# The last two weight pairs of an MLP's second linear by seven products too, in a fused LayerNorm, attention and MLP kernel

## Chip, cores and metric

One core of one Trainium2 chip. The metric is device time in microseconds of one execution, as the median of three runs. Numbers of the profile come from one further execution, taken by the hardware profiler.

## The reference

```
x = A_x                                   # [1, 2048, 576], fp32
xn = (x - mean(x)) / sqrt(var(x) + 1e-5)
qkv = xn @ wqkv                           # 32 heads of 18
# each token attends to 8 keys: itself and 7 earlier ones, 2 apart (masked before the start)
attn = softmax(q . k[pos - 2*w] / sqrt(18))
A = (sum over w of attn * v[pos - 2*w]) @ wo
h = xn @ w1 + b1                          # 576 -> 4608
B = (h * tanh(softplus(h))) @ w2          # Mish, 4608 -> 576
out = x + A + B
```

## The kernel before, in words

The 2048 tokens go in two halves of 1024 (hf 0 and 1), each in two blocks of 512. Every fp32 operand of a matmul is split in a high and a low part, so that one product takes three matmuls (high x high, high x low, low x high). The hidden 4608 columns go in 18 pairs q of 2 x 128 ("weight pairs"). Half 1 (hf = 0) prepares the weights: it loads them, splits them, and stores the split parts to DRAM (`keep`, `t_keep`); half 2 reads them back (`fetch`, `p_fetch`). Half 2 takes the pairs in the order Q1 = 1..17, 0, so the pair prepared first comes last.

Several products are done with seven half-size products in place of eight. In the second linear of half 2 this is done for groups of two pairs: the activations of the group form a 2 x 2 block matrix A11, A12, A21, A22 (by token block and 128 columns), the weights form B11, B21, B22 and four sums T1 to T4, and the left sides are A11, A12, A22 and four sums S1 to S4. Group e has seven "items" P1 to P7 in the order ORD = P7, P4, P1, P5, P2, P6, P3. For an item, `u_sum` makes the left sum in place, `u_high` (ACT) and `u_low` (DVE or POOL) split it into a unit u, `p_fetch` brings the weights (tile pw), and `p_item` does 24 matmuls 128x288 into four PSUM banks "po", which DVE adds to the sums accP. At the end `p_join` adds the seven sums up to the four outputs. Weight sums T1 to T4 are made in half 1 (`t_sum`, `t_high`, `t_low`, `t_keep`).

Eight groups (OC = 8) cover sixteen of the pairs. The last two pairs of half 2 (17 and 0) go by `m2_cols`: eight chunks of 24 matmuls, with split activations from `a_split`. Four of these chunks stand within the last pair, four after it, ahead of the output product with wo (`wo_part`, o_0 to o_7), whose left sides `o_split` transposes and splits.

Between the QKV products of half 2 and its first pair stands the z stage (`z_part`): the last QKV weights for four token blocks of 128, again by seven products. DVE adds their PSUM banks into zkv and zqs (`plus`), which frees the banks for the next products. At that time POOL and DVE also do the end of half 1's attention: POOL multiplies q by k (tiles pr_g_..), DVE reduces them to logits L, takes the maximum m and subtracts; then POOL multiplies by v (pv). POOL also makes sums s_62 to s_70 of the transposed input, which are split into S_1 and xt_1 (high and low) for later products.

The order of the program is set by a plan of slots: TensorE's work is a list of parts (`add`), and all else is put before a part by `before` and `put`, moved by a table MOVE of numbers by name; ON_VECTOR and ON_GPSIMD choose the engine of an addition. `spot(hf, q, i)` is a part within a pair; `at` finds a part. Attention is cut into steps spread over the parts that `ok` allows. Each engine runs its instructions strictly in program order. SP issues the DMAs. PSUM has four banks with tag "h" and four with tag "out".

Of the kernel before, what the change touches and what calls it, by code (L numbers as in the profile page):

```python
# [31 lines left out]
OC = 8  # L32
# [12 lines left out]
def block_kernel(ctx: ExitStack, tc: tile.TileContext, x, wq, wo, w1, b1, w2, mask, out):  # L45
# [239 lines left out]

    def fetch(kind, i):
        w = i
        if kind == "w2":
            w = 2 * Q1[i // 2] + i % 2
        elif kind != "wq":  # L290
            w = Q1[i]
# [410 lines left out]
    def prod(ph, wt, off, X, hi, lo, first, last):  # L702
        seq = [(off + k, wl, xs + k) for k in range(2) for wl, xs in ((0, hi), (0, lo), (1, hi))]
        for i, (wk, wl, xs) in enumerate(seq):
            nc.tensor.matmul(ph, wt[:, wl, wk * P:(wk + 1) * P], X[:, xs, :],  # L705
                             start=first and i == 0, stop=last and i == len(seq) - 1,
                             skip_group_check=True)
# [120 lines left out]

    def unit(e, k, qq):
        if (e, k, qq) not in units:  # L830
            units[e, k, qq] = sb.tile([P, 2, TB], F32R, tag=f"a{qq}", bufs=(3, 2)[qq], name=f"u_{e}_{k}_{qq}")
        return units[e, k, qq]

    def u_sum(e, k, qq):
        name, q = LEFT[ORD[k]], 2 * e + qq
        eng = engine(nc.gpsimd if (name, qq) in (("S1", 1), ("S4", 0)) else nc.vector, "u_sum", e, k, qq)
        x, y, op = dict(S3=("A11", "A21", ALU.subtract), S2=("A22", "S3", ALU.subtract), S1=("A11", "S2", ALU.add),
                        S4=("A12", "S2", ALU.subtract)).get(name, (None,) * 3)
        if x:
# [1 line left out]
            eng.tensor_tensor(out=t, in0=u_src(q, x), in1=u_src(q, y), op=op)
            held_[q, SLOT[name]] = name

    def u_high(e, k, qq):
        name, q = LEFT[ORD[k]], 2 * e + qq
        u = unit(e, k, qq)
        nc.scalar.copy(u[:, 0, :], u_src(q, name))

    def u_low(e, k, qq):
# [4 lines left out]
        eng.tensor_tensor(out=u[:, 1, :], in0=u_src(q, name),  # L854
                          in1=u[:, 0, :].bitcast(F32), op=ALU.subtract)

    def a_split(b, j):
        q = 2 * OC
        t = rawact[q, b, j]
        assert (q, f"A{b + 1}{j + 1}") in held_  # L860
        a = acts[1, q, b, j] = sb.tile([P, 2, TB], F32R, tag=f"a{b}", bufs=(3, 2)[b], name=f"act_1_{b}_{2 * q + j}")
        nc.scalar.copy(a[:, 0, :], t)
        nc.gpsimd.tensor_tensor(out=a[:, 1, :], in0=t, in1=a[:, 0, :].bitcast(F32), op=ALU.subtract)
# [50 lines left out]
    def m2_cols(hf, q, b, p):
        for c in range(2):
            for r_ in range(2):
                po = ps.tile([P, 512], F32, tag="out", bufs=4, name=f"po_{hf}_{q}_{b}_{p}_{c}_{r_}")[:, 0:HC]
# [643 lines left out]
```

## Time and profile before

| | |
|---|---|
| median of 3 runs | 1109.08 us (1108.84 to 1109.54) |
| profiled execution, own time | 1108.86 us |
| its span | 1106.9 us |
| granted TensorE clock, mean | 0.998 |
| TensorE busy | 1097.6 us, 6534 matmuls |
| VectorE (DVE) busy | 864.5 us |
| GpSimd (POOL) busy | 818.3 us |
| ScalarE (ACT) busy | 509.6 us |

The span is what the trace covers; some 2 us lie around it. PE is TensorE's matmuls, PEld its weight loads, which run beside them. In a row of groups, "out<-in" names the tiles, the shapes are partitions x elements, then follow the count, busy time, mean ns of one, and the idle time before with what ended it. In a timeline row stand the start, the time, the engine, the line and the operation.

### The profile page before, as it was taken

The page shows a single profiled execution, that of the slowest core. Times are in us where ns is not written, and L with a number is a line of the kernel's source. Part 1 is how long each engine was busy: PE and PEld are TensorE (multiplying, and loading weights), DVE is VectorE, ACT ScalarE, POOL GpSimd, SP SyncE. Part 2 cuts the span into 40 slices and gives each one's busy share as a digit, 9 for nine tenths or more (in the row PEclk, how much of TensorE's full clock was granted, in tenths as well). Part 3 has the DMA queues.
Part 4 walks back from the last instruction along what each step waited for, and adds up shares of the span by engine and source line. Part 5 has one row for each costly group of instructions (what it writes and reads, how often), then busy time and mean ns, then how long its engine had stood idle before and what let it go on. Part 6 is the DMA issues. An engine that isn't in the chain of part 4 may idle for free.

```text
span 1106.9 us, 18216 instructions
## 1 busy us (share of the span) xinstructions
PE 1097.6 (99%) x6534; PEld 1012.0 (91%) x6534; DVE 864.5 (78%) x1419; ACT 509.6 (46%) x933; POOL 818.3 (74%) x659
## 2 busy tenths in 40 slices
PE   9999999999999999999999999999999999999998
PEld 8999999999999999999998889989989899999998
DVE  6258699999899898988745466777878879897876
ACT  5544655545456456546332264534444443434232
POOL 4499899876577776895888559868696868699622
PEclk9999999999999999999999999999999999999999
DMA  6789897988889788878589497666567765675653
GB/s 237 259 272 322 281 317 257 315 309 308 288 276 349 245 299 287 295 252 305 199 299 353 124 361 283 229 242 235 185 223 279 245 234 196 227 245 201 215 186 104
DMA packets 162957, 286.10 MB, mean 258 GB/s; under 512 B 30994, under 2 KB 102708, under 8 KB 162868
## 3 DMA queue, kind: packets, MB, share of 16 engines
q1 hardware_dynamic: 162868, 284.95, 74.3%
q8 instruction: 51, 0.84, 0.3%
q14 instruction: 38, 0.31, 0.1%
HBM read 168.35 MB, written 116.55 MB: 257 GB/s over the span
## 4 chain that ended last, share of the span: by engine, by line
PE 91%; POOL 3%; DVE 2%; DMA 1%; ACT 1%; issue 1%; POOLq 0%; ACTq 0%
PE h L705 31%; PE po L808 21%; PE po L900 16%; PE pq L359 8%; PE h L711 6%; PE o L1041 4%; PE z L477 2%; PE po L921 2%; POOL s L656 1%; POOL pr L582 1%; DVE og L626 0%; POOL pv L620 0%; DMA q_d<-qs 0%; DMA o_d<-og 0%; POOL s_u L656 0%
## 5 line engine op out<-in xcount | busy, mean ns | idle before, releaser
L808 PEld LDWEIGHTS po<-w,act 128*128 128x128 f32 x1728 | 236.5, 188 | 5.6
L808 PE MATMUL po<-w,act 128*128 128x288 f32 x1728 | 240.6, 295 | 0.0
L582 POOL TENSOR_TENSOR pr<-q,kv 128x576 f32<-128x576 f32 x128 | 192.5, 1532 | 12.3 <-DVE og L626 12.0
L620 POOL TENSOR_TENSOR pv<-L,kv 128x576 f32<-128x576 f32 x128 | 172.7, 1451 | 36.3 <-DVE L L613 13.1
L900 PEld LDWEIGHTS po<-pw,u 128*128 128x128 f32 x1344 | 184.0, 188 | 5.1 <-DVE u L854 0.5
L900 PE MATMUL po<-pw,u 128*128 128x288 f32 x1344 | 187.1, 295 | 0.1
L359 PE MATMUL pq<-wq,xt 128*128 128x432 f32 x672 | 136.3, 361 | 1.4 <-ACT xt L92 1.2
L812 DVE TENSOR_TENSOR acc<-po,acc 128x288 f32<-128x288 f32 x288 | 116.4, 447 | 21.2 <-PE po L808 20.2
L359 PEld LDWEIGHTS pq<-wq,xt 128*128 128x128 f32 x672 | 125.0, 188 | 8.2 <-ACT xt L92 1.8
L906 DVE TENSOR_TENSOR accP<-po,accP 128x288 f32<-128x288 f32 x212 | 89.0, 450 | 33.0 <-PE po L900 28.8
L705 PE MATMUL h<-xt,t 128*128 128x512 f32 x432 | 110.6, 391 | 0.0
L705 PE MATMUL h<-S,t 128*128 128x512 f32 x432 | 110.4, 391 | 0.0
L626 DVE TENSOR_REDUCE og<-pv 128x144 f32<-128x1152 f32 x64 | 85.7, 1342 | 26.8 <-POOL pv L620 26.7
L705 PE MATMUL h<-xt,wa 128*128 128x512 f32 x432 | 104.2, 390 | 0.0
L587 DVE TENSOR_REDUCE L<-pr 128x64 f32<-128x1152 f32 x64 | 85.9, 1344 | 19.0 <-POOL pr L582 18.6
L705 PEld LDWEIGHTS h<-xt,wa 128*128 128x128 f32 x432 | 81.0, 188 | 17.2
L705 PEld LDWEIGHTS h<-xt,t 128*128 128x128 f32 x432 | 79.0, 188 | 15.0 <-DVE c L750 0.2
L705 PEld LDWEIGHTS h<-S,t 128*128 128x128 f32 x432 | 78.1, 188 | 13.0
L761 POOL TENSOR_TENSOR act<-c,act 128x512 fp32r<-128x512 f32 x38 | 53.2, 1402 | 33.0 <-ACT act L756 33.0
L751 ACT ACTIVATE c<-c,b1c 128x512 f32<-128x512 f32 x57 | 41.3, 724 | 68.1 <-DVE c L750 68.0
L739 ACT COPY c<-h 128x512 f32<-128x512 f32 x57 | 33.3, 584 | 54.7 <-PE h L705 29.7
L705 PE MATMUL h<-S,wc 128*128 128x512 f32 x216 | 55.7, 393 | 0.7 <-ACT rt L739 0.7
(275 smaller groups left out, 1937.4 us busy)
## 6 DMA issues: line engine op xcount, KB each, us to landing
kv<-kv_d SPq DMA_DIRECT2D x64, 396.0 KB, 5.4
kept_t<-t SPq DMA_DIRECT2D x36, 512.0 KB, 4.8
t<-kept_t SPq DMA_DIRECT2D x36, 512.0 KB, 5.8
pw<-kept_T SPq DMA_DIRECT2D x32, 576.0 KB, 5.2
kept_B<-w SPq DMA_DIRECT2D x48, 288.0 KB, 4.7
pw<-kept_B SPq DMA_DIRECT2D x24, 576.0 KB, 4.8
rw<-in_w SPq DMA_DIRECT2D x36, 320.0 KB, 5.1
kept_wa<-wa SPq DMA_DIRECT2D x18, 640.0 KB, 5.4
```

The costliest lines, as they stand in the source:

```text
L359: nc.tensor.matmul(pq[:, 0:432], XT[:, xi, tok], wt[wi][:, hl, 0:432], start=i == 0, stop=i == len(seq) - 1)
L582: nc.gpsimd.tensor_tensor(out=pr[:, x:x + hh], in0=q[:, j0 + x:j0 + x + hh, None, :].to_broadcast([P, hh, W, CU]), in1=win(kt, 0, CU, j0 + ...
L587: nc.vector.tensor_reduce(L[:, k, j0:j0 + hj].rearrange("p j w h -> p (j w h)"), pr.rearrange("p j w (h d) -> p (j w h) d", h=2), axis=AX, ...
L620: nc.gpsimd.tensor_tensor(out=pr[:, x:x + hj].rearrange("p j d w -> p j w d"), in0=L[:, k, x:x + hj, :, h:h + 1].to_broadcast([P, hj, W, DH]),
L626: nc.vector.tensor_reduce(og[:, :, c0:c0 + DH], pr, axis=AX, op=ALU.add)
L705: nc.tensor.matmul(ph, wt[:, wl, wk * P:(wk + 1) * P], X[:, xs, :], start=first and i == 0, stop=last and i == len(seq) - 1, skip_group_ch ...
L711: nc.tensor.matmul(ph, wt[:, wl, off * P:(off + 1) * P], X[:, xs, :], start=False, stop=wl == 1, skip_group_check=True)
L761: engine(nc.gpsimd, "act", n).tensor_tensor(out=a[:, 1, :], in0=t, in1=a[:, 0, :].bitcast(F32), op=ALU.subtract)
L808: nc.tensor.matmul(po, acts[hf, q, b, j][:, al, tok], done["w2", hf, 2 * q + j][:, wl, c * HC:(c + 1) * HC], start=i == 0, stop=i == 5)
L812: nc.vector.tensor_tensor(out=t, in0=po, in1=t, op=ALU.add)
L900: nc.tensor.matmul(po, units[e, k, qq][:, al, tok], w[:, qq, wl, :], start=i == 0, stop=i == 5)
L906: nc.vector.tensor_tensor(out=t, in0=po, in1=t, op=ALU.add)
```

## The change

The ninth group. OC becomes 9, so the pairs 17 and 0 go by seven items as the others do, in an order of their own (LAST), and `m2_cols` and `a_split` go. All seven stand behind the last pair's first linear, four of them ahead of the transposes of `o_split`'s first steps and three behind.

```
-OC = 8
+OC = 9
...
-    seven = lambda hf, q: hf == 1 and q <= 2 * OC
+    seven = lambda hf, q: hf == 1
...
+    LAST = ("P1", "P4", "P7", "P5", "P2", "P6", "P3")
+    def nth(e, k):
+        return (LAST if e == OC - 1 else ORD)[k]
...
-    for k in range(4):
-        pr_(1, NP - 1, *CHUNKS[k])
+    while len(items) < 7 * OC:
+        pi()
...
+            if e == OC - 1:
+                ds = dict(P1=(0, -6, -5), P4=(0, -4, -3), P7=(-3, -2, -2), P5=(-2, -1, -1), P2=(0, -2, -2), P6=(-2, -2, -2),
+                          P3=(-3, -2, -1))[nth(e, k)]
...
-    for n, (a, b) in enumerate((("P6", "P1"), ("P7", "P6"), ("P6", "P5"), ("P2", "P1"), ("P3", "P6"), ("P4", "P7"), ("P5", "P7"))):
+    for n, (a, b) in enumerate((("P2", "P1"), ("P6", "P1"), ("P7", "P6"), ("P6", "P5"), ("P4", "P7"), ("P5", "P7"), ("P3", "P6"))):
         for pr in range(2):
...
+            i = items[-1][2] - 1 + (0, 0, 1, 1, 2, 3, 4)[n]
```

The weights of these pairs are now prepared as those of the others: sums T1 to T4 of the pairs 17 and 0 in half 1, kept in DRAM. Pair 0's w2 rows are loaded a second time for that, late in half 1 (`load_again`, at spot(0, 14, 8)), and its sums made at spot(0, 15, 8).

```
+    def load_again(i):
+        t = again["w2", i] = sb.tile([P, 5 * P], F32, tag="xn", bufs=XNB, name=f"again_{i}")[:, 0:D]
+        nc.sync.dma_start(t, w2[i * P:(i + 1) * P, :])
...
-    for q in range(1, 2 * OC + 1):
-        i = spot(0, q, (3,2)[q > 1])
+    for k in range(2):
+        before(spot(0, 14, 8) + k, lambda k=k: load_again(k))
+    for q in range(NP):
+        i = spot(0, q, (3, 2)[q > 1]) if q else spot(0, 15, 8)
```

Besides, o tiles 0 to 3 of the first half go to other buffers and are loaded within the last pair, wo's second part is fetched from the ninth group's third item on, attention steps may stand at every part of half 2, and the tables are set anew:

```
+    for i in range(spot(1, 0, 0), len(plan)):
+        ok[i] = True
...
-MOVE = {"0 s_high": -6, "0 s_low": 18, "0 s_step": 3, ...
+MOVE = {..., "u_sum 8 0 0": 77, "u_sum 8 0 1": 66, ...
```

**The tail on TensorE.** Before, these rows stand around the first transposes of `o_split` (ot_0), between the fourth and fifth chunk of the last pair; po_17 is a chunk's bank:

```order
L921 MATMUL po_17_1_1_1_1_11727<-w_1_0_11441,act_1_0_11564 128x288 x3
L921 MATMUL po_17_1_1_1_1_11727<-w_1_1_11368,act_1_1_11515 128x288 x3
L955 MATMUL ot_0_11740<-ident,o_1_11617 128x128 x4
L971 MATMUL ot_0_11741<-ident,o_0_11612 128x128 x4
L973 MATMUL ot_0_11742<-ident,o_0_11612 128x128
L973 MATMUL ot_0_11742<-ident,o_1_11617 128x128
L921 MATMUL po_17_0_0_0_0_11766<-w_1_0_11441,act_0_0_11396 128x288 x3
L921 MATMUL po_17_0_0_0_0_11766<-w_1_1_11368,act_0_1_11623 128x288 x3
```

After, the transposes stand between the fourth item (P5, po_3) and the fifth (P2, po_4) of the ninth group; the left sides come as weights pw against units u:

```order
L898 MATMUL po_3_1_1_11692<-pw_3_11481,u_3_0_11619 128x288 x3
L898 MATMUL po_3_1_1_11692<-pw_3_11481,u_3_1_11624 128x288 x3
L942 MATMUL ot_0_11710<-ident,o_1_11359 128x128 x4
L958 MATMUL ot_0_11711<-ident,o_0_11324 128x128 x4
L960 MATMUL ot_0_11712<-ident,o_0_11324 128x128
L960 MATMUL ot_0_11712<-ident,o_1_11359 128x128
L898 MATMUL po_4_0_0_11742<-pw_4_11664,u_4_0_11546 128x288 x3
L898 MATMUL po_4_0_0_11742<-pw_4_11664,u_4_1_11660 128x288 x3
```

With the seven items, 168 matmuls take the place of 192; the last pair's first linear before them is as it was.

**The z stage on DVE.** Before, from the second reduction of the logits of group 7 to the additions of token block 1 (z_1; the banks 7190 are the second product's):

```order
L587 TENSOR_REDUCE L_7_7111<-pr_7_0_1_7142 128x64
L587 TENSOR_REDUCE L_7_7111<-pr_7_1_0_7183 128x64
L490 TENSOR_TENSOR zkv_0_7082<-z_1_7192,zkv_0_7082 128x8x36
L490 TENSOR_TENSOR zqs_0_7083<-z_1_7192,zqs_0_7083 128x4x36
L587 TENSOR_REDUCE L_7_7111<-pr_7_1_1_7187 128x64
L597 TENSOR_TENSOR L_7_7111<-L_7_7111,mk 2x256
L601 TENSOR_REDUCE m_7_7217<-L_7_7111 128x32
L603 TENSOR_TENSOR L_7_7111<-L_7_7111,m_7_7217 128x256
L490 TENSOR_TENSOR zkv_1_7088<-z_1_7190,zkv_1_7088 128x8x36
L490 TENSOR_TENSOR zqs_1_7089<-z_1_7190,zqs_1_7089 128x4x36
```

After, from the first addition of token block 0 on:

```order
L491 TENSOR_TENSOR zqs_0_7126<-z_0_7135,zqs_0_7126 128x4x36
L588 TENSOR_REDUCE L_7_7024<-pr_7_0_1_7120 128x64
L588 TENSOR_REDUCE L_7_7024<-pr_7_1_0_7175 128x64
L491 TENSOR_TENSOR zkv_1_7131<-z_0_7133,zkv_1_7131 128x8x36
L491 TENSOR_TENSOR zqs_1_7132<-z_0_7133,zqs_1_7132 128x4x36
L491 TENSOR_TENSOR zkv_1_7127<-z_0_7134,zkv_1_7127 128x8x36
L491 TENSOR_TENSOR zqs_1_7128<-z_0_7134,zqs_1_7128 128x4x36
L588 TENSOR_REDUCE L_7_7024<-pr_7_1_1_7179 128x64
L598 TENSOR_TENSOR L_7_7024<-L_7_7024,mk 2x256
L602 TENSOR_REDUCE m_7_7219<-L_7_7024 128x32
L604 TENSOR_TENSOR L_7_7024<-L_7_7024,m_7_7219 128x256
L491 TENSOR_TENSOR zkv_0_7125<-z_1_7236,zkv_0_7125 128x8x36
```

All four reductions stand one token block earlier: two of them are now ahead of the additions of z_0's banks, and the last, with the maximum and the subtraction, is ahead of z_1's first bank.

**The z stage on POOL.** Before, from s_69 to the last products of group 7:

```order
L656 TENSOR_TENSOR s_69_7028<-xt_0_6249,s_68_7022 128x512
L656 TENSOR_TENSOR s_69_7028<-s_69_7028,xt_0_6249 128x512
L582 TENSOR_TENSOR pr_7_0_0_7114<-q_14_6864,kv_0_14_6862 128x576 x2
L692 TENSOR_TENSOR S_1_6866<-s_69_7028,S_1_6866 128x2x256
L656 TENSOR_TENSOR s_70_7120<-xt_0_6249,xt_1_6637 128x512
L656 TENSOR_TENSOR s_u_7121<-xt_0_6249,xt_1_6637 128x512
L656 TENSOR_TENSOR s_70_7120<-s_70_7120,s_u_7121 128x512
L582 TENSOR_TENSOR pr_7_0_1_7142<-q_14_6864,kv_0_14_6862 128x576 x2
L582 TENSOR_TENSOR pr_7_1_0_7183<-q_15_6876,kv_0_15_6874 128x576 x2
L582 TENSOR_TENSOR pr_7_1_1_7187<-q_15_6876,kv_0_15_6874 128x576 x2
```

After, from the end of s_68:

```order
L657 TENSOR_TENSOR s_68_7000<-s_66_6995,xt_0_6289 128x512
L657 TENSOR_TENSOR s_68_7000<-s_68_7000,xt_0_6289 128x512
L583 TENSOR_TENSOR pr_7_0_0_7027<-q_14_6878,kv_0_14_6876 128x576 x2
L583 TENSOR_TENSOR pr_7_0_1_7120<-q_14_6878,kv_0_14_6876 128x576 x2
L583 TENSOR_TENSOR pr_7_1_0_7175<-q_15_6910,kv_0_15_6908 128x576 x2
L583 TENSOR_TENSOR pr_7_1_1_7179<-q_15_6910,kv_0_15_6908 128x576 x2
L657 TENSOR_TENSOR s_69_7182<-xt_0_6289,s_68_7000 128x512
L657 TENSOR_TENSOR s_69_7182<-s_69_7182,xt_0_6289 128x512
L693 TENSOR_TENSOR S_1_6846<-s_69_7182,S_1_6846 128x2x256
L657 TENSOR_TENSOR s_70_7274<-xt_0_6289,xt_1_6687 128x512
```

The products of group 7 now run one after the other, and s_69, its low part S_1 and s_70 stand behind them.

**The tail on DVE.** Before, the rows that end the last chunks (L924) with `o_split`'s (L984, L985, L981) between, and the first of wo:

```order
L924 TENSOR_TENSOR accP_0_7691<-po_17_0_0_1_0_11782,accP_0_7691 128x288
L924 TENSOR_TENSOR accP_0_7691<-po_17_0_0_1_1_11790,accP_0_7691 128x288
L984 TENSOR_TENSOR s_0_11749<-ot_0_11741,s_0_11759 128x256
L985 TENSOR_TENSOR ob_11738<-ot_0_11742,ob_11738 64x256
L981 TENSOR_TENSOR oa_11737<-ot_0_11741,oa_11737 128x512
L924 TENSOR_TENSOR accP_1_7686<-po_17_0_1_0_0_11804,accP_1_7686 128x288
L924 TENSOR_TENSOR accP_1_7686<-po_17_0_1_0_1_11812,accP_1_7686 128x288
L924 TENSOR_TENSOR accP_1_7692<-po_17_0_1_1_0_11820,accP_1_7692 128x288
L924 TENSOR_TENSOR accP_1_7692<-po_17_0_1_1_1_11828,accP_1_7692 128x288
L1045 TENSOR_TENSOR y_11615<-o_0_11847,y_11615 128x288
```

After, the rows from P6's evictions (po_5) to the first of wo:

```order
L904 TENSOR_TENSOR accP_0_8079<-po_5_0_1_11789,accP_0_8079 128x288
L904 TENSOR_TENSOR accP_1_8096<-po_5_1_0_11797,accP_1_8096 128x288
L904 TENSOR_TENSOR accP_1_8096<-po_5_1_1_11805,accP_1_8096 128x288
L907 TENSOR_TENSOR accP_1_7638<-accP_1_7638,accP_1_7866 128x576
L907 TENSOR_TENSOR accP_1_7755<-accP_1_7755,accP_1_8096 128x576
L904 TENSOR_TENSOR accP_0_7643<-po_6_0_0_11819,accP_0_7643 128x288
L904 TENSOR_TENSOR accP_0_7643<-po_6_0_1_11827,accP_0_7643 128x288
L904 TENSOR_TENSOR accP_1_7644<-po_6_1_0_11835,accP_1_7644 128x288
L904 TENSOR_TENSOR accP_1_7644<-po_6_1_1_11843,accP_1_7644 128x288
L971 TENSOR_TENSOR s_0_11719<-ot_0_11711,s_0_11734 128x256
L972 TENSOR_TENSOR ob_11708<-ot_0_11712,ob_11708 64x256
L1032 TENSOR_TENSOR y_11851<-o_0_11869,y_11851 128x288
```

Two joins (L907) now stand between the evictions of P6 and of P3, and `o_split`'s last rows (L971, L972) behind P3's.

More of the change, by code (lines that the diff above doesn't have):

```diff
@@ L270, in keep @@
         t = done[kind, 0, i]
-        if kind == "w2" and 1 <= i // 2 <= 2 * OC:
-            e, qq = divmod(i // 2 - 1, 2)
+        if kind == "w2":
+            e, qq = divmod((i // 2 - 1) % NP, 2)
             names = ("B21", "B22") if i % 2 else ("B11",)
@@ L286, in fetch @@
     def fetch(kind, i):
[L287 to L291, printed above, removed]
+        w = Q1[i] if kind != "wq" else i
         t = done[kind, 1, i] = new(kind, 1, w)
@@ L325, in t_keep @@
     def t_keep(q, name):
-        e, qq = divmod(q - 1, 2)
+        e, qq = divmod((q - 1) % NP, 2)
         if (name, e) not in kept:
@@ L855, in u_low @@
                           in1=u[:, 0, :].bitcast(F32), op=ALU.subtract)
[L857 to L863, printed above, removed]
     def p_fetch(e, k):
-        name = RIGHT[ORD[k]]
+        name = RIGHT[nth(e, k)]
         t = pw[e, k] = sb.tile([P, 2, 2, HC], F32R, tag="w2", bufs=4, name=f"pw_{e}_{k}")
@@ L888, in p_item @@
     def p_item(e, k):
-        name = ORD[k]
+        name = nth(e, k)
         w = pw[e, k]
@@ L912, in c_out @@
         return pacc[("P2", "P3", "P4", "P5")[2 * b + c], pr]
[L914 to L917, printed above, removed]
-                tok = slice((2 * p + r_) * P, (2 * p + r_ + 1) * P)
-                for i in range(6):
-                    j, (al, wl) = i // 3, ((0, 0), (0, 1), (1, 0))[i % 3]
-                    nc.tensor.matmul(po, acts[hf, q, b, j][:, al, tok],
-                                     done["w2", hf, 2 * q + j][:, wl, c * HC:(c + 1) * HC], start=i == 0, stop=i == 5)
-                t = c_out(b, c, p)[:, r_]
-                nc.vector.tensor_tensor(out=t, in0=po, in1=t, op=ALU.add)
     oTs = {}
@@ L931, in o_load @@
             return
-        o = os_[hf, j] = sb.tile([P, 5 * P], F32, tag="xn", bufs=XNB, name=f"o_{hf}_{j}")
+        tag, bufs = ("xn", XNB) if hf or j > 3 else (("raw", 4), ("w2", 4))[j // 2]
+        o = os_[hf, j] = sb.tile([P, 5 * P], F32, tag=tag, bufs=bufs, name=f"o_{hf}_{j}")
         ov = o_d[hf].rearrange("(p j) d -> p j d", j=TJ)[:, j, :]
@@ L1026, in wo_part @@
         A, B, S = od["A"], od["B"], od["S"]
-        ts = [ys[j + k][:, 0:D] for k in range(2)] if hf == 0 else None
+        ts = lambda k: ys[j + k][:, 0:D]
         ov = out[hf * SH:(hf + 1) * SH, :].rearrange("(p j) d -> p j d", j=TJ)
@@ L1043, in acc @@
         def acc(k, c, h):
-            t = c_out(j // JB, c, j % JB // 2)[:, k] if hf else ts[k][:, c * HC:(c + 1) * HC]
+            t = c_out(j // JB, c, j % JB // 2)[:, k] if hf else ts(k)[:, c * HC:(c + 1) * HC]
             nc.vector.tensor_tensor(out=t, in0=h, in1=t, op=ALU.add)
@@ L1145, in end @@
                     y_store(b * JB + jj)
-        add(("p", hf, q, b, p), lambda: ((m2_cols if hf else m2_pair)(hf, q, b, p), end()), alias=alias)
+        add(("p", hf, q, b, p), lambda: (m2_pair(hf, q, b, p), end()), alias=alias)
     items = []
@@ L1234, in quad @@
                     pi()
-                elif part == "C":
-                    pr_(1, q - 1, *C9.pop(0))
                 else:
-                    for p_ in {4:(3,)}.get(part, ()) if q == 1 else ():
+                    for p_ in {4: (3,)}.get(part, ()) if q == 1 else ():
                         zi(JB - 1, p_)
@@ L1387, in block_kernel @@
             before(ps_[kind], lambda kind=kind, q=q: fetch(kind, q))
-        for j in range(2):
-            if q >= 2 * OC:
-                before(spot(1, q, 0 if q else 3) + j, lambda q=q, j=j: fetch("w2", 2 * q + j))
     assert len(items) == 7 * OC, items
@@ L1465, in block_kernel @@
                 ok[spot(hf, q, i)] = i in ((0, 3, 7, 9), (0, 3, 5, 7, 9))[hf] and (q > 1 or i)
-    for q in range(2 * OC + 2):
-        for i in range(spot(1, q, 0), spot(1, q, 9) + 1):
-            ok[i] = True
-    marks = [at["q", 0, 2, 0, 1], at["q", 0, 3, 0, 0], spot(0, 1, 0), spot(0, 2 * OC + 1, 0), at["q", 1, 0, 0, 0], at["z", 0, 0], spot(1, 0, 0),
+    for i in range(spot(1, 0, 0), len(plan)):
+        ok[i] = True
+    marks = [at["q", 0, 2, 0, 1], at["q", 0, 3, 0, 0], spot(0, 1, 0), spot(0, NP - 1, 0), at["q", 1, 0, 0, 0], at["z", 0, 0], spot(1, 0, 0),
              spot(1, 2, 0), spot(1, NP - 1, 0), at["o", 0, 0], at["o", 2, 0]]
@@ L1496, in block_kernel @@
         before(i + 2 + n, lambda name=name: wo_fetch(name))
-    j = at["p", 1, NP - 1, 1, 0]
+    j = items[7 * (OC - 1) + 2][2]
     before(j, lambda: wo_home(1))
@@ L1501, in block_kernel @@
     for k in range(2):
-        before(j + -1, lambda k=k: (o_load(0, k), y_load(k)))
+        before(spot(1, NP - 1, 2 * k), lambda k=k: o_load(0, k))
+        before(j + 2, lambda k=k: y_load(k))
         before(at["o", 0, 0], lambda k=k: (o_load(0, 2 + k), y_load(2 + k)))
```

39 lines of the change are left out of this document (15 added, 24 removed).

## Prediction

> **What bounds the kernel now.** I read the head of the page first, then TensorE's groups, then the waits of TensorE, then the clock around the longest of them. The span, the busy times and the chain by engine:
>
> ```profile
> span 1106.9 us, 18216 instructions
> PE 1097.6 (99%) x6534; PEld 1012.0 (91%) x6534; DVE 864.5 (78%) x1419; ACT 509.6 (46%) x933; POOL 818.3 (74%) x659
> PE 91%; POOL 3%; DVE 2%; DMA 1%; ACT 1%; issue 1%; POOLq 0%; ACTq 0%
> ```
>
> TensorE is busy for all but 9.3 us of 1106.9 us. So time goes away in two ways only: fewer matmuls, or fewer waits and slow stretches of TensorE. The other engines matter where TensorE waits for them. All such waits (us in total, times, longest):
>
> ```profile
> PE z L477 <- DVE zqs L490: 1.8, 1, 1.8
> PE warm L76 <- POOL ident masks.py:199: 1.3, 1, 1.3
> PE pq L359 <- ACT xt L92: 1.2, 2, 0.6
> PE h L705 <- ACT rt L739: 0.7, 1, 0.7
> PE o L1041 <- DVE y L1045: 0.6, 1, 0.6
> PE pq L359 <- POOL wq L1158: 0.2, 1, 0.2
> ```
>
> The longest stands in the z stage. TensorE's rows there (start, us, count, idle before), and the granted clock in slices of 1 us (the column after POOL's count):
>
> ```profile
> 586.52 2.52 PE L477 MATMUL z<-zacc_B,xt 128*128 128x432 f32 x12
> 596.49 2.52 PE L477 MATMUL z<-zacc_B,xt 128*128 128x432 f32 x12
> ...
> 606.72 1.69 PE L477 MATMUL z<-z_B,S 128*128 128x432 f32 x6 [1.82 <-DVE zqs L490]
> ...
> 608.92 3.53 PE L477 MATMUL z<-zacc_B,xt 128*128 128x432 f32 x12
> 619.75 2.52 PE L477 MATMUL z<-zacc_B,xt 128*128 128x432 f32 x12
> ```
> ```profile
> 607.00:608.00 1.00, 1.00 (x6) 0.92 (x6) 0.93 (x5) 0.00 (x0) 0.00 (x0) 0.88 0.99 372
> 608.00:609.00 1.00, 1.00 (x5) 0.91 (x4) 0.42 (x1) 0.00 (x0) 0.35 (x1) 0.50 0.41 151
> 609.00:610.00 1.00, 1.00 (x4) 0.92 (x3) 0.00 (x0) 0.58 (x2) 1.00 (x2) 0.50 0.09 35
> 610.00:611.00 1.00, 1.00 (x4) 0.93 (x3) 0.00 (x0) 0.00 (x0) 1.00 (x2) 0.50 0.01 2
> 611.00:612.00 1.00, 1.00 (x6) 0.94 (x6) 0.92 (x1) 0.58 (x2) 1.00 (x2) 0.92 0.00 0
> 636.00:638.00 2.00, 1.42 (x6) 1.20 (x7) 2.00 (x3) 1.97 (x3) 2.00 (x2) 1.00 1.13 257
> ```
>
> The wait of 1.82 us is followed by some 3.4 us at half clock (0.12 + 3 x 0.50 + 0.08 = 1.70 us lost); the wait of 0.7 us in the last row left the clock at 1.00. The four token blocks of this stage start with the same x12 group: they are 596.49 - 586.52 = 9.97, 12.43 and 10.83 us apart. Against the undisturbed 9.97 the excess is 2.46 + 0.86 = 3.32 us. That is the price of this one wait, nearly twice what the table of waits shows.
>
> The Trainium skill, "TensorE: Matmul & The Clock Gate" (Part 1: The HAM clock gate), has the clock go to half after an idle window of about 3.4 us and back after as long a busy one. The length of the slow stretch agrees with the rows; the trigger doesn't, since 1.82 us of idling sufficed. By the rule's trigger the slow rows would have another cause, the wait would be worth 1.82 us alone, and the sum below would end 1.5 us higher.
>
> **The change, part by part.**
>
> *Matmuls.* The last two pairs went by eight chunks of 24 matmuls, and go by seven items of 24; every other TensorE row keeps its count. One block costs what the rows of these two lines and the chain of waits give:
>
> ```profile
> L900 PE MATMUL po<-pw,u 128*128 128x288 f32 x1344 | 187.1, 295 | 0.1
> L921 PE MATMUL po<-w,act 128*128 128x288 f32 x192 | 26.3, 295 | 0.0
> 1009.39 3.18 PE po L921 x24
> ```
>
> Items and chunks have the same form and duration; 192 become 168, so 24 go: -3.17 us (24 x 0.132 us of issue, as the chain's block shows). Nothing covers that; it is on the path.
>
> *The z stage.* In before, DVE reaches the additions that free the banks of token block 1 only behind the reduction of pr_7_1_1 and three softmax rows; POOL ends those products late:
>
> ```profile
> 583.63 1.29 POOL L656 TENSOR_TENSOR s<-xt,s 128x512 f32<-128x512 f32 x1
> 585.00 1.62 POOL L656 TENSOR_TENSOR s<-s,xt 128x512 f32<-128x512 f32 x1
> 586.57 2.82 POOL L582 TENSOR_TENSOR pr<-q,kv 128x576 f32<-128x576 f32 x2
> 589.35 1.75 POOL L692 TENSOR_TENSOR S<-s,S 128x512 fp32r<-128x512 f32 x1
> ...
> 594.93 8.40 POOL L582 TENSOR_TENSOR pr<-q,kv 128x576 f32<-128x576 f32 x6
> 603.37 1.35 DVE L587 TENSOR_REDUCE L<-pr 128x64 f32<-128x1152 f32 x1 [0.86 <-POOL pr L582]
> 606.00 0.45 DVE L490 TENSOR_TENSOR zkv<-z,zkv 128x288 f32<-128x288 f32 x1
> ```
>
> In the new order s_69, S_1 and s_70 stand behind the products. Those four pieces were 583.63 to 586.57 and 589.35 to 594.93 us, so the products start about 2.9 us earlier and run through: 8 x 1.40 = 11.2 us from 583.6, ending near 594.8 instead of 603.3. The last reduction and its softmax rows (1.35 + 1.3 us) are over near 597.5, seven us ahead of 604.9, where TensorE asked. That wait goes, with its slow stretch: -3.32 us. Late next is token block 0: two reductions now stand ahead of its additions. The third pair of products ends near 583.6 + 8.4 = 592.0, its reduction near 593.4, the first two additions (0.45 + 0.30) near 594.2; TensorE needs them near 594.9. The margin is about 0.8 us. The sums put behind the products feed xt_1 for block 2, ready near 607.5 against a need near 610.
>
> *The tail.* Rows of one form stand for the added work: 14 u_high and u_low in place of 8 splits, the sums, and the seven joins:
>
> ```profile
> 1011.60 1.54 DVE L924 TENSOR_TENSOR accP<-po,accP 128x288 f32<-128x288 f32 x4
> 1000.73 0.68 DVE L854 TENSOR_TENSOR u<-rm,u 128x512 fp32r<-128x512 f32 x1
> 994.55 1.48 DVE L854 TENSOR_TENSOR u<-ra_r,u 128x512 fp32r<-128x512 f32 x1
> L841 DVE TENSOR_TENSOR rm<-ra,rm 128x512 f32<-128x512 f32 x8 | 8.7, 1085 | 0.8 <-ACT rm L751 0.8
> 1007.08 2.52 DVE L909 TENSOR_TENSOR accP<-accP,accP 128x576 f32<-128x576 f32 x2
> 1038.71 0.41 DVE L984 TENSOR_TENSOR s<-ot,s 128x256 f32<-128x256 f32 x1
> 1041.31 1.75 PE L1041 MATMUL o<-wo,oa 128*128 128x288 f32 x12
> ```
>
> From the last item of group eight to the first wo matmul TensorE has about 28 us, and o_0 would start at 1041.31 - 3.17 = 1038.1 (the z stage's gain left out of this count). DVE has in it 32 evictions (8 x 1.54 = 12.3), 6 u_low (4.1 at 0.68, 8.9 at 1.48), 3 u_sum (3.3), one reduction (1.35), 7 rows of o_split (3.2) and two joins (2.52): 26.7 to 33.6 us. I take 0.68, since POOL, whose attention ends some 15 us earlier in the new order, leaves DVE mostly alone there; then each u is ready 0.8 us or more ahead of its item (the closest is P7's second, through DVE, POOL, ACT and POOL in turn). But the two joins stand ahead of P3's four evictions and of the o_split row that frees the third bank of o_0: P6's evictions end near 1035.4, the joins 1037.9, P3's evictions 1039.5, that row 1039.9; TensorE is there at 1038.1 plus half of 1.75, 1039.0. So +0.9 us, call it +1.0; 0 if DVE is a little ahead, +5.6 if the upper sum holds.
>
> The Trainium skill, "SBUF — State Buffer" (SBUF: two separate sides), gives DVE operations with two SBUF inputs and GpSimd one shared port pair, held for a whole instruction. The 0.68 and 1.48 of the same row form fit that. By it the price of a u_low is set by whether POOL is in an operation, and with POOL in one throughout the tail's sum would be its upper end.
>
> *The slots.* Half 1 takes on T sums for two more pairs (4 sums, 4 halves, 4 stores) and all other work is placed anew. TensorE had no idle time there, but DVE had little room:
>
> ```profile
> 163.00:524.00 361.00, 361.00 (x2192) 330.79 (x2191) 330.05 (x538) 195.78 (x320) 274.54 (x232) 1.00 0.84 292
> 211.08:235.50 24.42, 24.42 (x148) 22.12 (x147) 23.91 (x39) 11.57 (x20) 19.77 (x17) 1.00 1.03 375
> 476.80:500.90 24.10, 24.10 (x147) 22.10 (x147) 19.07 (x23) 10.34 (x17) 23.16 (x21) 1.00 0.70 243
> ```
>
> The new sums fall in the last four pairs, where DVE (the last row) had 5 us free in 24; about 4 us each there, so covered. Elsewhere a pair's DVE load reaches 23.91 of 24.42 us, and a wait is possible wherever a row slips by more than the rest. I put +0.3, between nothing and one stall like the one above (3.3). In the prologue five wq halves go to DVE ahead of the statistics, so xn_4 comes about 2 us later, just when its transposes want it: +0.3 (0 to 0.6, as the waits for xt). Each fetch of pw is issued a few items ahead as for groups one to eight: nothing.
>
> Sum: -3.17 - 3.32 + 1.0 + 0.3 + 0.3 = -4.9. The profiled execution took 1108.86 us (span 1106.9 and 2.0 around it), 0.22 under the median of 1109.08. From the median: 1104.2.
>
> **The rivals.**
>
> *The stall moves to z_0.* If POOL reaches pr_7_0_0 more than 0.8 us later than I count, the reductions hold back token block 0, and at 1.8 us the clock halves too: 1104.2 + 3.3 = 1107.5. For it: a thin margin from a count by hand. Against: 8.5 us gained, 7 of them free.
>
> *A new stall in half 1*: a DVE row in a pair at 98% slips past TensorE's need, once: +3.3 us, 1107.5; twice, 1110.8. For it: the second window above. Against: before had none at the same load.
>
> *The tail is DVE-bound* (the slower side). With u_low at 1.48 and evictions spread, DVE needs 33.6 us in 28: P2, P6, P3 and o_0 each find their banks full. That is 5.6 us, and two of the four waits pass the length that halves the clock (2 x 1.70): 9.0 in place of the 1.0. 1104.2 + 8.0 = 1112.2. It decides against the change from 8.7 us on (the gain of 6.5 and 2.2). For it: the thin sum. Against: POOL's attention is over by then.
>
> *The half clock has another cause than the wait*: the z stage gives 1.82, and the time is 1105.7. This is what the clock page's trigger would say; against it, the slow rows begin a microsecond after the wait and nowhere else in the middle.
>
> *The matmuls don't fall*: excluded, the rows on TensorE are 24 matmuls fewer.
>
> **How the numbers follow.** Forecast 0.53; z_0 0.13; half 1 0.17; tail 0.10; other cause 0.07. 0.2% (2.2 us) is about what a measurement of this kernel can tell from no change, so faster ends at 1106.9. The forecast and the last count as faster (0.60), as do the z_0 and half-1 cases with waits too short to halve the clock (0.08): 0.68. The rest of these two is within 0.2% but for two stalls at once (0.02): 0.20. Slower: 0.12. The range: below, all gains at no price, and the 0.7 and 0.6 us waits gone as well: 1109.1 - 6.5 - 1.3 = 1101.3. Above, the two stall cases and another 2 us of tail, 1109.5. Beyond it lie the DVE-bound tail and double stalls. The forecast's own range is 1102.5 to 1106.
>
> **What would show it.** Matmuls 6534 - 24 = 6510 in the page. No wait of L491 on DVE over 0.3 us, clock 1.00 in the z stage, its four blocks 10 us apart. In the tail: P items back to back at 3.17 us, then one wait of about 1 us at o_0's third bank, on DVE (L971 or L972). Wrong would be a clock below 1.00 anywhere in the middle, waits of P items on u or on evictions, or a new wait of h on DVE in half 1.

## The result, and the profile after

The changed kernel takes 1106.18 us, the median of 20 runs (1102.09 to 1108.96), against 1109.24 for the kernel before, 20 runs too. The ratio is 0.995 (0.9927 to 0.9972): 5.5 us, with an interval of 3.1 to 8.1. The ratio compares runs that stand side by side and so differs a little from that of the two medians. Left out of all comparisons are two executions that were slow as a whole, one of the repeat below (1338.89 us, mean clock 0.753) and one of before (2201.66 us). The times of the changed kernel are not one cloud. Eight of the 20 lie at 1102.1 to 1103.1 us with a granted clock of 0.999 or 1.00, twelve at 1105.1 to 1109.0, ten of these with a clock of 0.997 or 0.998. The median lies in the lower part of the upper group. The profiled execution is of the upper group: 1108.94 us, span 1106.8. The head of its page:

```profile
span 1106.8 us, 18262 instructions
PE 1096.2 (99%) x6510; PEld 1009.7 (91%) x6510; DVE 862.5 (78%) x1425; ACT 516.4 (47%) x943; POOL 837.1 (76%) x675
```

There are 24 matmuls fewer, as the change says, and yet the span is 0.1 us from that of before. The waits of TensorE in this execution (us in total, times, longest) say why:

```profile
PE h L706 <- DVE rm L751: 2.8, 1, 2.8
...
PE z L478 <- ACT zkv L487: 0.6, 1, 0.6
PE h L706 <- DVE c L751: 0.3, 1, 0.3
PE z L478 <- DMA z_B<-kept_wq: 0.3, 1, 0.3
...
```

The lines left out are waits that before had too. The wait of 1.82 us for `zqs` is gone, and so is the 0.6 us for `y` at the end. In their place stands one of 2.8 us of a first linear (h) for `rm`, which no term of the sum has, one of 0.3 us for `c`, and two short ones in the z stage. That stage, in the timeline (start, us, engine, line, count, idle before and its releaser):

```profile
583.82 12.10 POOL L583 TENSOR_TENSOR pr<-q,kv 128x576 f32<-128x576 f32 x8
587.47 2.52 PE L478 MATMUL z<-zacc_B,xt 128*128 128x432 f32 x12
593.28 0.83 PE L478 MATMUL z<-z_T,S 128*128 128x432 f32 x3 [0.55 <-ACT zkv L487]
597.54 0.85 PE L478 MATMUL z<-z_B,S 128*128 128x432 f32 x3 [0.28 <-DMA z_B<-kept_wq]
598.63 2.50 PE L478 MATMUL z<-zacc_B,xt 128*128 128x432 f32 x12
608.44 2.52 PE L478 MATMUL z<-zacc_B,xt 128*128 128x432 f32 x12
618.27 2.52 PE L478 MATMUL z<-zacc_B,xt 128*128 128x432 f32 x12
```

POOL's eight products run unbroken from 583.8 to 595.9, and the blocks stand 11.16, 9.81 and 9.83 us apart: 30.80 us in all, where before had 33.23. So the stage gave 2.43 us. The two new waits took 0.83 of it, so what went with the old stall is put at 3.26.

Half 2's fourth pair is where it was lost again. TensorE's row there, then DVE's and POOL's of the microseconds before, then the clock in slices of 1 us (the column after POOL's count; the slices left out are at 0.50):

```profile
680.40 2.93 PE L706 MATMUL h<-xt,wa 128*128 128x512 f32 x6 [2.79 <-DVE rm L751]
```
```profile
671.05 7.24 DVE L860 TENSOR_TENSOR u<-rm,u 128x512 fp32r<-128x512 f32 x1 [2.16 <-ACT u L853]
678.21 1.54 DVE L904 TENSOR_TENSOR accP<-po,accP 128x288 f32<-128x288 f32 x4
679.67 0.68 DVE L751 TENSOR_TENSOR rm<-h,rm 128x512 f32<-128x512 f32 x1
...
668.12 2.82 POOL L583 TENSOR_TENSOR pr<-q,kv 128x576 f32<-128x576 f32 x2
670.91 2.80 POOL L884 TENSOR_TENSOR accP<-accP,accP 128x576 f32<-128x576 f32 x2
673.68 2.82 POOL L583 TENSOR_TENSOR pr<-q,kv 128x576 f32<-128x576 f32 x2
676.46 1.27 POOL L860 TENSOR_TENSOR u<-ra,u 128x512 fp32r<-128x512 f32 x1
```
```profile
679.00:680.00 1.00, 0.00 (x0) 0.00 (x0) 1.00 (x4) 0.00 (x0) 0.00 (x0) 0.84 1.04 423
680.00:681.00 1.00, 0.60 (x2) 0.50 (x3) 1.00 (x3) 0.62 (x1) 0.00 (x0) 0.50 0.89 365
...
686.00:687.00 1.00, 1.00 (x5) 0.73 (x5) 0.24 (x1) 0.24 (x1) 1.00 (x1) 0.75 0.00 0
```

One subtraction of DVE (the low part `u_low` of a unit u, L860: two inputs in SBUF), which takes 0.68 us at its shortest, stands from 671.05 to 678.29. POOL's rows shown run without a gap from 668.12 to 677.73, five operations of them beside the subtraction, and the subtraction ends 0.56 us after the last. Behind it on DVE stand the evictions of P5 and the addition `rm` that frees the bank TensorE wants. TensorE idles 2.79 us and then finds half the clock up to some 686.5; from 680.4 on that is about 6.1 us at half speed, 3.05 lost. The stall costs 5.8 us in all, and the execution without it would have a span of 1101.0, where the lower group has 1100.0 to 1101.0.

The tail, DVE's and TensorE's rows from the two joins (L907) on:

```profile
1039.31 1.93 DVE L907 TENSOR_TENSOR accP<-accP,accP 128x576 f32<-128x576 f32 x2
...
1043.06 0.43 DVE L972 TENSOR_TENSOR ob<-ot,ob 64x256 fp32r<-64x256 f32 x1
...
1041.91 1.76 PE L1028 MATMUL o<-wo,oa 128*128 128x288 f32 x12
1043.54 0.53 PE L1028 MATMUL o<-wo_r,ob 128*128 128x288 f32 x2
```

TensorE waits nowhere in it. P3's evictions, left out, end at 1042.70. DVE's row `ob` ends at 1043.49, and the matmul that reads it starts at 1043.54.

### The profile page after: what moved, and what is told of

Same layout as the page of the kernel before. It is cut to its first block, busy times and chain, and to the rows that moved or that the text cites. A ratio compares the mean times of both kernels' runs of the same rounds, so it can differ in the third digit from the quotient of the medians.

```text
span 1106.8 us, 18262 instructions
## 1 busy us (share of the span) xinstructions
PE 1096.2 (99%) x6510; PEld 1009.7 (91%) x6510; DVE 862.5 (78%) x1425; ACT 516.4 (47%) x943; POOL 837.1 (76%) x675
## 4 chain that ended last, share of the span: by engine, by line
PE 96%; DVE 1%; DMA 1%; issue 1%; ACT 0%; DVEq 0%
PE h L706 31%; PE po L809 20%; PE po L898 18%; PE pq L360 11%; PE h L712 6%; PE o L1028 5%; PE z L478 3%; DMA z_B<-kept_wq 1%; PE ta L86 0%; PE ot L942 0%; PE ot L958 0%; DMA acc<-in_x 0%; DVE st L123 0%; PE ot L960 0%; DVE accP L904 0%
## 5 line engine op out<-in xcount | busy, mean ns | idle before, releaser
L898 PEld LDWEIGHTS po<-pw,u 128*128 128x128 f32 x1512 | 206.6, 188 | 4.7
L898 PE MATMUL po<-pw,u 128*128 128x288 f32 x1512 | 209.6, 295 | 0.0
L621 POOL TENSOR_TENSOR pv<-L,kv 128x576 f32<-128x576 f32 x128 | 176.4, 1480 | 27.3 <-ACT rt L740 16.0
L813 DVE TENSOR_TENSOR acc<-po,acc 128x288 f32<-128x288 f32 x288 | 118.7, 448 | 32.9 <-PE po L809 31.7
L904 DVE TENSOR_TENSOR accP<-po,accP 128x288 f32<-128x288 f32 x240 | 101.2, 450 | 41.2 <-PE po L898 40.2
L762 POOL TENSOR_TENSOR act<-c,act 128x512 fp32r<-128x512 f32 x28 | 38.8, 1388 | 41.5 <-ACT act L757 41.2
L860 POOL TENSOR_TENSOR u<-rm,u 128x512 fp32r<-128x512 f32 x29 | 40.5, 1400 | 23.4 <-ACT u L853 23.4
```

The lines of the kernel that those rows point to most:

```text
L621: nc.gpsimd.tensor_tensor(out=pr[:, x:x + hj].rearrange("p j d w -> p j w d"), in0=L[:, k, x:x + hj, :, h:h + 1].to_broadcast([P, hj, W, DH]),
L813: nc.vector.tensor_tensor(out=t, in0=po, in1=t, op=ALU.add)
L898: nc.tensor.matmul(po, units[e, k, qq][:, al, tok], w[:, qq, wl, :], start=i == 0, stop=i == 5)
L904: nc.vector.tensor_tensor(out=t, in0=po, in1=t, op=ALU.add)
```

## The experiments

Two questions: what is the stall, and why does only a part of the executions have it; and how large were the terms of the sum by themselves? My theory is that the `u_low` was kept from SBUF by POOL's unbroken row. The rival is that DVE was merely loaded so that its evictions came late, and that the two groups of times have another cause.

**The changed kernel once more**, unedited.

> The changed kernel once more, nothing edited. Its times so far lie in two groups, 1102.1 to 1103.1 and 1105 to 1109 us, and its profiled execution (span 1106.8) lost 5.9 us at one place: the low part of unit u_4_1 of group 0 on DVE took 7.24 us beside an unbroken row of five POOL operations, TensorE waited 2.79 us for the DVE row behind it, and ran at half clock for 6.8 us after that. Theory (DVE is locked out while POOL runs back to back, by chance of timing): the two groups again; an execution with a mean clock of 1.00 spans 1100 to 1101 us and shows no DVE operation over 2.5 us at this place; one of 1105 us and more shows the long row here, or at another place with a wait of TensorE behind it. Rival (DVE waits there for a DMA or a semaphore, the x_send tiles): the long row is there in each execution, at a length that goes with the DMA.

Its five other times were 1102.12, 1102.21 and 1103.39 with a clock of 1.00, and 1107.24 and 1107.79 with 0.998: both groups again, in one program on one chip. Ratio 0.9954 (0.9936 to 0.9972). The profiled execution is of the lower group, 1103.39 us with a span of 1101.3. DVE's and POOL's rows at the same place:

```profile
671.50 1.77 DVE L860 TENSOR_TENSOR u<-rm,u 128x512 fp32r<-128x512 f32 x1 [2.17 <-ACT u L853]
...
675.34 0.68 DVE L751 TENSOR_TENSOR rm<-h,rm 128x512 f32<-128x512 f32 x1
...
671.29 3.27 POOL L884 TENSOR_TENSOR accP<-accP,accP 128x576 f32<-128x576 f32 x2
```

The same subtraction, beside the same row of POOL, started 0.45 us later (POOL's sum started 0.38 us later as well) and took 1.77 us; it got in after one operation of POOL. `rm` follows at 675.34 in place of 679.67, and there is no wait. The work is the same, so load alone is not the difference. In the same profile another DVE subtraction with two inputs in SBUF (L428, at 278.05 us) took 4.74 us beside four operations of POOL, so such a row can come elsewhere too.

**The subtraction later on DVE.** One number of the slot table: `u_low` of P5's second unit goes behind P5's evictions and the two additions that free h's banks.

```diff
-MOVE = {... "u_low 0 4 1": -16, ...}
+MOVE = {... "u_low 0 4 1": -10, ...}
```

> As the changed kernel, but the low part of u_4_1 of group 0 stands on DVE behind the four evictions of P5 and the two additions that TensorE waits for (rm, ra), in place of ahead of them. Nothing else moves. Lockout theory: whatever the length of that operation, TensorE no longer waits there; median 1102.5, all executions within 1102 to 1103.5 unless a lockout falls at another exposed place. Rival (the evictions themselves wait for x_send's DMA or for x_diff on POOL): the wait of h on DVE stays, median as for the changed kernel, near 1106.

Measured: 1102.87 us, the median of five (1102.58 to 1103.49), ratio 0.994 (0.9927 to 0.9953); the upper group is gone. DVE's rows there:

```profile
671.95 0.99 DVE L904 TENSOR_TENSOR accP<-po,accP 128x288 f32<-128x288 f32 x2 [3.47 <-POOL accP L884]
674.44 0.68 DVE L751 TENSOR_TENSOR rm<-h,rm 128x512 f32<-128x512 f32 x1
675.64 2.86 DVE L860 TENSOR_TENSOR u<-rm,u 128x512 fp32r<-128x512 f32 x2
```

The evictions now wait for POOL's sum in accP (3.47 us), harmlessly: `rm` still comes at 674.44. DVE has as much to do as in the unedited kernel.

**The subtraction on POOL.** The same `u_low` is done by POOL, ahead of its sum; DVE is rid of it.

```diff
-ON_GPSIMD = ("d_low w T1", ...)
+ON_GPSIMD = ("u_low 0 4 1", "d_low w T1", ...)
```

> As the changed kernel, but the low part of u_4_1 of group 0 is done by POOL, ahead of x_diff, so that DVE has no operation with two SBUF inputs beside POOL's row. Lockout theory: DVE's evictions follow TensorE at once, no wait of h, median 1102.5 to 1103.5 (POOL's row is 1.3 us longer, and x_diff and P5's evictions come that much later). Rival (DMA or x_diff): the wait stays or grows by the 1.3 us, near 1107.

Measured: 1103.29 us (1101.81 to 1103.46), ratio 0.9939 (0.9927 to 0.9951), and TensorE has no wait for `rm`. Two different ways round that one instruction end at the lower group, ten executions of ten, where the unedited kernel had 14 of 25 in the upper. So the second group is this instruction's doing. The stall itself was seen in one profile; that the others of the upper group have it at the same place is inferred from these ten. Two of the 14, 1105.12 and 1105.70 us with clocks of 1.00 and 0.999, have less of the half clock or none, and nothing on record shows what they waited for.

**The z stage alone.** The kernel before, with only the three slots that put the sums s_70 behind the products of group 7:

```diff
-MOVE = {... "s_high 1 3": -15, "s_low 1 3": -2, "s_step 1 3": -7, ...}
+MOVE = {... "s_high 1 3": 2, "s_low 1 3": -3, "s_step 1 3": 23, ...}
```

> The kernel before with one thing of the change alone: the sums s_70 (three POOL operations) stand behind the products of group 7 in place of ahead of them (the numbers of s_step, s_high and s_low for 1 3). My term: DVE reaches the additions of token block 1 some 2 us before TensorE asks, the wait of 1.82 us and the 3.4 us at half clock behind it go: 1109.1 - 3.3 = 1105.8, the four z blocks near 10.0 us apart, clock 1.00 there. Rival (the half clock has another cause than the wait): only 1.8 us less, 1107.3, the clock still 0.5 near 608 us. Rival (the wait moves to another bank of the z stage): 1109.

Measured: 1107.3 us (9 runs, 1106.15 to 1108.84) against 1110.13 for before beside it, ratio 0.9978 (0.9969 to 0.9988): 2.4 us by the ratio (1.3 to 3.4), 2.8 by the medians. TensorE's rows, and the slice of the clock that was at 0.88 to 0.50 in before:

```profile
587.34 2.52 PE L477 MATMUL z<-zacc_B,xt 128*128 128x432 f32 x12
597.59 2.50 PE L477 MATMUL z<-zacc_B,xt 128*128 128x432 f32 x12
606.30 1.43 PE L477 MATMUL z<-z_B,S 128*128 128x432 f32 x6 [0.29 <-DVE zqs L490]
607.97 2.50 PE L477 MATMUL z<-zacc_B,xt 128*128 128x432 f32 x12
617.78 2.52 PE L477 MATMUL z<-zacc_B,xt 128*128 128x432 f32 x12
```
```profile
607.00:608.00 1.00, 1.00 (x7) 0.96 (x6) 0.93 (x3) 0.00 (x0) 0.99 (x1) 1.00 1.04 397
```

The blocks are 10.25, 10.38 and 9.81 us apart, 30.44 in place of 33.23: 2.79 us less. A wait of 0.29 is left. With the long wait the half clock is gone too, so the rival of another cause falls.

**The block of 24 matmuls.** The late-subtraction kernel, with the last item's 24 matmuls done twice, the second time over the first:

```diff
-                for i in range(6):
+                for i in range(12 if (e, k) == (OC - 1, 6) else 6):
+                    i %= 6
```

> e1_late_u with the 24 matmuls of the last item (P3 of the ninth group) done twice, the second time over the first. Nothing else is added. My term for the removed block: a block on TensorE in the tail is on the path at its full length, so +3.17 us over e1_late_u (median 1102.87): 1106.0. Rival (the tail is bound by DVE, which the longer item gives time to catch up): less than 3.17, down to +2 us.

Measured: 1106.23 us (8 runs, 1105.45 to 1106.8); ratio to before 0.9965 (0.994 to 0.999). That is 3.36 above the 1102.87 of the kernel it was made from, but on another chip, where before took 1108.81 us in place of 1110.13, so the medians give the difference to a microsecond or so. The profiles are closer. TensorE's items after the transposes and the first wo matmuls, in the late-subtraction kernel and with the block twice:

```profile
1025.97 9.76 PE L898 MATMUL po<-pw,u 128*128 128x288 f32 x72
1035.57 1.76 PE L1028 MATMUL o<-wo,oa 128*128 128x288 f32 x12
```
```profile
1026.72 12.93 PE L899 MATMUL po<-pw,u 128*128 128x288 f32 x96
1039.50 1.76 PE L1029 MATMUL o<-wo,oa 128*128 128x288 f32 x12
```

From the first item to wo are 9.60 us and 12.78 us: 3.18 for 24 matmuls, so the 3.17 of the rows holds.

**The tail's slack.** The late-subtraction kernel, with reductions of 128x1024 (results unused) on DVE between the joins and P3's evictions: one, then two.

```diff
+        for _ in range(1 if (e, k) == (OC - 1, 6) else 0):    # 2 in the other
+            nc.vector.tensor_reduce(spare, ident[:, None, :].to_broadcast([P, 8, P]), ...)
```

> e1_late_u with one more DVE reduction (128x1024, about 1.2 us) between the two joins and the evictions of P3. In e1_late_u the o_split row that TensorE needs (ob) ended 0.06 us ahead of the matmuls that read it (wo_r x ob, the 13th of o_0). If that margin is the whole slack of the tail, TensorE waits some 1.1 us there, the clock stays at 1.00, and the time is +1.1 us: 1104.0. Rival (more slack than one row shows): no wait, 1102.9.

> e1_late_u with two such reductions (2.4 us) at the same place. If only the wait counts: +2.3, 1105.2. If a wait over 1.8 us halves the clock for 3.4 us and more behind it, as in the z stage before: +2.3 + 1.7 at least, 1106.9 or more.

TensorE's row that waits, with one and with two:

```profile
1040.19 0.54 PE L1030 MATMUL o<-wo_r,ob 128*128 128x288 f32 x2 [1.00 <-DVE ob L974]
```
```profile
1040.64 0.53 PE L1030 MATMUL o<-wo_r,ob 128*128 128x288 f32 x2 [2.26 <-DVE ob L974]
```

The waits are 1.00 and 2.26 us. By the medians, again across two chips, one cost 0.9 us (1103.79, 4 runs, 1102.95 to 1105.59) and two cost 3.2 (1106.07, 10 runs, 1104.58 to 1107.7); ratios to before 0.9956 (0.994 to 0.9972) and 0.9979 (0.997 to 0.9988). Nearly the whole of each reduction (1.13 and 2.38 us on DVE up to P3's evictions) comes out as a wait, so the tail had no slack to speak of, 0.1 us at most. With two, four of the ten executions, the profiled one among them, had a clock of 1.00 (median 1105.9) and six had 0.997 or 0.998 (median 1106.8). So the same program can halve the clock there or not.

**The clock and the port by themselves.** A small kernel leaves out all of the computation. TensorE runs bursts of 90 matmuls with idle gaps of varied length between; then POOL multiplies 48 times without a gap while DVE does small work with two inputs in SBUF.

```python
for k in range(48):
    nc.gpsimd.tensor_tensor(out=pr[k % 4], in0=xs[6 + k % 3], in1=xs[9 + k % 2], op=ALU.mult)
nc.vector.tensor_tensor(out=d[:, 0:8], in0=link, in1=link, op=ALU.add)
```

> A small kernel by itself; it leaves out the whole computation (the output is x). First part: bursts of 90 matmuls (12 us) with idle times of TensorE between them that DVE sets, an eviction (0.45 us), 0 to 9 reductions of 0.4 us and one subtraction (0.7 us), in mixed order. From the rows so far, idle times up to 0.7 us keep the clock at 1.00, 1.82 us halved it for 3.4 us and 2.79 us for 6.8 us. Theory A (a threshold between 0.7 and 1.8 us): each idle time above it halves the clock, each below doesn't. Theory B (a window that runs by itself, so that the same idle time sometimes does and sometimes doesn't): mixed results between about 1.0 and 3 us, and slow stretches of one or two times 3.4 us. Second part: POOL does 48 multiplications 128x576 back to back, while DVE does subtractions 128x512 with both inputs in SBUF, one after every two to four reductions; then the same with one DVE input in PSUM. Lockout theory: with both inputs in SBUF a subtraction waits for the POOL operation that is running (0.7 to 2.1 us) and now and then through several of them (3 us and more); with one input in PSUM none takes over its own 0.45 us. Rival (DVE and POOL slow each other down by bandwidth): all take some 1.4 us, in both parts.

TensorE's rows behind three of the gaps (a burst takes 12.12 us at full clock), and the clock around the first and the last:

```profile
51.77 13.65 PE L45 MATMUL po<-g,wt 128*128 128x288 f32 x90 [2.84 <-DVE g L49]
...
115.12 14.75 PE L45 MATMUL po<-g,wt 128*128 128x288 f32 x90 [4.66 <-DVE g L49]
132.25 12.13 PE L45 MATMUL po<-g,wt 128*128 128x288 f32 x90 [2.38 <-DVE g L49]
```
```profile
52.69:56.10 3.41, 3.41 (x17) 3.41 (x16) 0.00 (x0) 0.00 (x0) 0.00 (x0) 0.50 0.57 179
132.00:136.00 4.00, 3.75 (x28) 3.75 (x29) 0.19 (x1) 0.00 (x0) 0.00 (x0) 1.00 0.00 0
```

Gaps of 1.15, 1.48, 1.93 and 2.38 us left the clock at 1.00, six from 2.84 to 4.20 halved it for one stretch of 3.41 us, 4.66 and 5.11 for two. The slow stretches begin and end at whole multiples of 3.413 us from one another (52.69, 56.10, 83.41, 86.82, 114.13, 120.96 us and so on), whatever the gap: a grid, which lies elsewhere in each trace (1.49 us off the multiples of 3.413 from the start here, 0.18 in before, where the slow stretch begins at 607.75). In this trace a stretch of that grid at full clock with at most 0.39 of it idle is followed by full clock, one with 0.73 or more by half. A slow stretch in which TensorE was busy throughout is followed by full clock; the two that began with TensorE idle (0.29 and 0.38 of them, behind the gaps of 4.66 and 5.11 us) were followed by a second slow one. In the kernel before, the 1.82 us lie within one stretch, 0.53 of it, and halved the next. The 2.26 us above lie across a border, 0.32 and 0.34 of two stretches, and the 2.38 us with 0.39 and 0.31. That explains why a wait of 1.8 is slow in one kernel and 2.26 or 2.38 is not in another: it counts how it lies to the grid, and a threshold on the wait alone (theory A) falls.

The port, DVE's rows (the group of subtractions, mean in ns, then one small addition) and POOL's second row:

```profile
L62 DVE TENSOR_TENSOR d<-x,x 128x512 f32<-128x512 f32 x20 | 23.0, 1149 | 0.0
```
```profile
363.77 64.95 DVE L59 TENSOR_TENSOR d<-link 128x8 f32<-128x8 f32 x1 [27.28 <-POOL link L56]
...
363.70 65.00 POOL L58 TENSOR_TENSOR pr<-x,x 128x576 f32<-128x576 f32 x48
```

Twenty subtractions got in after one operation of POOL at the most (0.68 to 1.84 us each), and the same addition of 8 columns ahead of POOL's first row took 1.34 us. Ahead of the second it did not get in until the row was over, 64.95 us later. So the long case is rare, and it can last to the end of POOL's row. What decides between the two stays open. A control with one input in PSUM was meant to run beside POOL too, but it was queued behind that one addition, and so nothing is shown by it.

## Why the prediction was right, and where it was not

1104.2 was forecast and 1106.18 measured: faster, and inside the range. How near the two lie is luck: the times fall in two groups, neither at 1104.2, and the median depends on how many of the 20 fell in the upper. The prediction's own sign of being wrong, a clock below 1.00 in the middle, did appear. By its steps:

- **Matmuls, -3.17: right.** 6510 of them, and 3.18 us on TensorE when put back.
- **The z stage, -3.32: right in place and mechanism, a little large.** The stall returned 3.26, the stage as a whole 2.43 in the changed kernel and 2.79 alone. Token block 0, with its margin of 0.8 us, did not wait for DVE, and that rival fell; its matmuls waited 0.55 us for ACT (`zkv`, L487) and 0.28 for a transfer instead. The row of POOL ended 1.1 us later than I counted, since its eight products took 12.1 and not 11.2.
- **The half clock follows the wait: right**, and the rival of another cause fell with the z stage alone. The runs show that a stretch of the grid idle for a little over half can do, 0.53 of it in before and not 0.39; and that 2.38 us across a border did nothing. "TensorE: Matmul & The Clock Gate" of the Trainium skill (Part 1: The HAM clock gate) asks for an idle window, and 1.82 us did not fill one.
- **The tail, +1.0: mis-sized, it is 0, and wrong in its place.** I had the joins at 2.52 us, from a row beside POOL; they took 1.93. I named o_0's third bank, the seventh matmul; what depends on DVE's last row there is the thirteenth (`wo_r` by `ob`), 0.9 us later. It has a margin of 0.05 us, which the added reductions found. The DVE-bound tail fell. Its upper sum was also added up wrongly: with u_low at 1.48 the terms listed give 31.6 us and not 33.6, so that rival was priced 2 us too high. In addition the 0.6 us wait for `y` went, which the sum left in.
- **Half 1 and the prologue, +0.6: about right.** The profiled execution had 0.95 us of it ahead of the z stage, among it 0.3 us for `c` on DVE.
- **The step that failed is "a new stall": its kind was right, its place and cause were not.** The rival had a wait and a half clock, +3.3, in half 1, from DVE's load. It came in half 2, at 5.8 us (a wait of 2.79 and some 3.05 of half clock, since the first of its two slow stretches began with TensorE idle), from one instruction held back by POOL, in about half the executions. I had read the 0.68 and the 1.48 of one row form as the port's two prices ("SBUF — State Buffer" of the Trainium skill, SBUF: two separate sides) and took 1.48 for the upper one. A third price was in the trace of before, which I had not looked for: the first row below, of its timeline, a low part of a first-linear weight. POOL's rows beside it have no gap, and it ends 0.56 us after the last of them, as the 7.24 us did. TensorE did not wait for it.

```profile
494.45 6.77 DVE L266 TENSOR_TENSOR t<-tt,t 128x512 fp32r<-128x512 f32 x1
...
493.61 1.46 POOL L323 TENSOR_TENSOR twT<-twT,twhT 128x576 fp32r<-128x576 f32 x1
495.01 2.84 POOL L582 TENSOR_TENSOR pr<-q,kv 128x576 f32<-128x576 f32 x2
497.79 1.45 POOL L323 TENSOR_TENSOR twT<-twT,twhT 128x576 fp32r<-128x576 f32 x1
499.17 0.25 POOL L151 COPY xn<-xn 128x64 f32<-128x64 f32 x1
499.36 1.30 POOL L761 TENSOR_TENSOR act<-c,act 128x512 fp32r<-128x512 f32 x1
```

The sum for the profiled execution: -3.17 of matmuls, -2.43 of z, -0.6 of `y`, +0.95 ahead of z and +5.8 of the stall are +0.55, and the span moved by -0.1; the remaining -0.65 I could not place. Without the stall that is -5.9, and the lower group (mean 1102.7) is 6.5 under before.

Moving the subtraction is the version that beats both kernels: 1102.87 us against 1110.13 for before and a mean of 1104.55 for the five times of the change in its repeat, all on the same chip.

## What to carry to other kernels

When GpSimd runs several operations without a gap, put every VectorE operation with two SBUF inputs that nobody needs soon behind the evictions that TensorE waits for: mostly it costs an operation's length, but now and then the whole row, and everything queued behind it. Price a TensorE wait of 1.8 us and more as the wait and then 1.5 to 1.7 us for each stretch of half clock (3.32 - 1.82 in the z stage, 13.65 - 12.12 in the small kernel, 3.05 for 6.1 us behind the stall), and note that the same wait may come without it. Read the single times before the median: two groups with two clocks point to an event that happens in some executions only, and profiles of one execution of each group, laid side by side, can show it.

## What the runs showed of the hardware that I had not expected

- A VectorE operation with two SBUF inputs can be kept out through 5, 6 or 48 operations of GpSimd in a row (7.24, 6.77 and 64.95 us). That is rare: in the nine profiles of the large kernels two more exceed 2.3 us, 4.74 in the repeat and 5.38 in the z stage alone (495.25 us, the instruction of the 6.77 again).
- The granted clock changed only on a grid of 3.413 us, whatever the gap. Over half a stretch idle (0.53) was enough to halve the next, 0.39 was not; a slow stretch that began with idle time was followed by another (4.66 and 5.11 us of gap gave 6.83 us of half clock, 2.84 to 4.20 gave 3.41).
- So a wait of 2.26 us cost itself alone in one execution, while one of 1.82 cost 3.3.
